# Batch 1 of an attention and MoE kernel: scores and strided turns issued at earlier steps, one subtraction moved from GpSimd to VectorE

## The chip, the cores and the metric

The kernel runs on one core of one Trainium2 chip. The metric is the device time of one execution in microseconds (us), and the time of a kernel is the median of its runs. A core has five engines that run side by side and meet at semaphores: TensorE (PE in the profile; PEld is its weight load), VectorE (DVE), ScalarE (ACT), GpSimd (POOL) and SyncE (SP). Matmul results land in PSUM, from where VectorE or ScalarE take them to SBUF. Here all loads are issued from GpSimd's queue, all stores from SyncE's.

## The reference

Two stages follow each other. The first is attention with a window, for 8 batches, 8 heads, 576 positions and head size 64:

```python
scores = scale * np.matmul(q, k.transpose(0, 1, 3, 2))
rel = pos[:, None] - pos[None, :]
mask_plain = (rel >= 0) & (rel < window)                                   # heads 0 to 3, window 32
mask_dil = (rel >= 0) & (rel < window * dilation) & (rel % dilation == 0)  # heads 4 to 7, dilation 4
scores = np.where(masks, scores, -1e9); scores -= max; attn = exp(scores)
attn = attn / (sum(attn) + 1e-9);  x = attn @ v
```

The second is a feed-forward layer over all 4608 tokens (8 batches of 576), with 512 features and 2048 hidden units: `h = x @ w_in`, `g = h * sigmoid(h)` (SiLU), `out = g @ w_out`.

## The kernel before

**Two kinds of work, one stream.** The feed-forward layer fills TensorE: for each batch `layer1` (L715) runs 16 steps of 8 matmuls (L721) and ScalarE applies SiLU to each (L729). `layer2` (L778) then runs 16 matmuls (L790) for each output tile of 128 tokens, VectorE copies the tile out of PSUM (`store`, L773, the copy at L775) and SyncE stores it. An odd batch such as batch 1 has five output tiles, numbers 4 to 8. The attention of later batches is woven into this stream.

**The steps.** `plan_of(b)` (L816) lists which piece of attention work is issued at which step while batch b's feed-forward layer runs. Steps 0 to 15 are the 16 steps of `layer1`. From step 16 on a step is four matmuls of `layer2`: tile 4 has steps 16 to 19, tile 5 has 20 to 23, tile 6 has 24 to 27, tile 7 has 28 to 31, tile 8 has 32 to 35. The pieces of a step are issued ahead of that step's matmuls. Nothing is sorted afterwards: each engine runs its instructions in the order in which the program issues them (the schedule is manual), and waits at the first whose inputs or buffers aren't ready. So a step number fixes an instruction's place in the order of every engine that it uses.

**The attention of one batch.** z = 0 stands for the plain heads, z = 1 for the strided (dilated) ones.

1. `load_qk`, `load_v`: q, k, v come in through GpSimd's queue, in tiles n0 (q), n1 (k) and vw. One `load_squares` issues four DMAs (L152).
2. `transposes(at, b, z, step)` (L801): q and k are turned so that the head size lies on partitions. Batch 2's plain heads are turned on TensorE, with copies on VectorE and ScalarE (L287). Batch 2's strided heads and everything of batch 3 are turned on VectorE by `turn_qk` (L329): two stream transposes each, kC and qC at L337 (strided), kT and qT at L335 (plain). `transposes` also passes two copy engines, which only the turn on TensorE uses.
3. `scores(b, z)` (L494): 72 (plain) or 80 (strided) small matmuls (L364 or L374) into PSUM tiles s and ss. Then VectorE scales and masks them into a tile ms (L408, three or four instructions) and takes the maxima (L488, two instructions). Each z has two halves, hi = 0 and 1, with a tile ms each. There are five buffers for ms, so the sixth tile waits until the first has been read.
4. `exps(b, z, hi)` (L548): ScalarE takes exponentials, as 8 or 10 small instructions with sums (L568), one per block of 64 keys. Where `shift` (L538) has subtracted the maximum from the whole tile before, it's one instruction (L557), and VectorE sums later (L576).
5. `later` (L808) places `normal` (L581: r at L587 and L588, the product pn at L590), `turned` (L594: a stream transpose into pt, L606), `values` (L647: matmuls of pt with v, L637) and `finish` (L663, copies into xT).

**Around the change.** In batch 1, batch 2's plain halves are normalized at steps 22 and 24, and their `values` are issued at step 28, ahead of tile 7; the strided ones follow at 29, 30 and 34. `values` starts with 28 matmuls that need only the first half of pt; the others need the second. ScalarE takes all 38 small exponentials of batch 2 after its last SiLU of batch 1, behind a load of its function table. In the kernel before, `shift(3, 0, 0)` is given `nc.gpsimd`, and runs on GpSimd behind batch 4's load instructions, which are issued at step 17. Output tiles o use two PSUM buffers (`big`): tile 6 may start when VectorE has copied tile 4, and tile 8 when it has copied tile 6.

The lines that the change and the prediction name are: L329 `turn_qk`, L494 `scores`, L538 `shift`, L548 `exps`, L581 `normal`, L594 `turned`, L773 `store` and L850 to L865, the plan of batch 1.

Of the kernel before, what the change touches and what calls it, by code (L numbers as in the profile page):

```python
# [29 lines left out]
def kernel(  # L30
# [9 lines left out]
    nc = tc.nc  # L40
# [212 lines left out]
    def att(b):  # L253
        if b not in state:
            state[b] = {
                "qT": qTs[b % 2],
                "kT": kTs[b % 2],
                "qC": qCs[b % 2],
                "kC": kCs[b % 2],
                "vw": vws[b % 2],  # L260
                "pt": {},
                "xT": [xtp.tile([P, 2, S], F16, tag=f"xT{z}", name=f"xT_{b}_{z}") for z in (0, 1)],
            }
        return state[b]
# [134 lines left out]
    def width(b, z, g):  # L399

        if b == 0:
            return 8 + g * (4 if z else 2)
        return 10 if z or g else 8
# [131 lines left out]
                masked(ms[:, 8:10], ss[0], band_of(2))  # L535
            reduce_max(b, z, m, ms)

    def shift(b, z, hi, engine=nc.vector):  # L538

        a = att(b)  # L540
        w = width(b, z, hi)
        ms, nm = a["ms", z, hi], a["nm", z, hi]
        engine.tensor_tensor(
            ms[:, 0:w], ms[:, 0:w], nm[:, 0:w, None].broadcast_to([P, w, KB]), ALU.add
        )
        a["shifted", z, hi] = True
# [251 lines left out]
    dve, act = nc.vector.tensor_copy, nc.scalar.copy  # L798
    both = (dve, act)

    def transposes(at, b, z, step, copies=both):  # L801
        for which in (1, 0):
            if b >= DT[z]:
                at(step, turn_qk, b, z, which)
                continue
            at(step, transpose, b, z, which, copies)

    def later(at, b, z, steps, copies=(nc.vector.tensor_copy, nc.vector.tensor_copy)):  # L808

        for hi in (0, 1):  # L810
            at(steps[hi], normal, b, z, hi)
            at(steps[hi], turned, b, z, hi)
        at(steps[3], values, b, z)
        at(steps[3], finish, b, z, copies)

    def plan_of(b):  # L816
        ev = {}

        def at(s, fn, *args):
            ev.setdefault(s, []).append((fn, args))  # L820

        def all_exps(b, z):
            for hi in (0, 1):
                at(16, exps, b, z, hi)

        if b == 0:

            at(-8, values0, 1, 1)
            at(-8, finish0, 1, 1, (act, dve))
            at(-6, values0, 0, 1)  # L830
            at(-6, finish0, 0, 1)
            at(0, build_mask)
            at(1, load_qk, 2)
            transposes(at, 1, 1, 4)
            at(8, scores, 1, 1, 0)
            at(10, scores, 1, 1, 1)
            at(12, transpose, 1, 0, 1, both)
            at(14, transpose, 1, 0, 0, both)
            at(10, shift, 1, 1, 0)
            at(16, scores, 1, 0, 0)  # L840
            at(18, scores, 1, 0, 1)
            at(18, shift, 1, 0, 1)
            at(15, load_qk, 3)
            at(15, load_v, 2)
            all_exps(1, 1)
            for hi in (0, 1):
                at(20, exps, 1, 0, hi)
            later(at, 1, 1, (20, 21, 24, 27), (act, act))
            later(at, 1, 0, (23, 24, 28, 31), (act, act))
        elif b == 1:  # L850
            at(16, load_v, 3)
            transposes(at, 2, 0, 3)
            transposes(at, 2, 1, 10)
            transposes(at, 3, 0, 17, (dve, dve))
            at(8, scores, 2, 0)
            at(17, load_qk, 4)
            at(13, scores, 2, 1)
            all_exps(2, 0)
            all_exps(2, 1)
            at(20, scores, 3, 0)  # L860
            at(21, shift, 3, 0, 0, nc.gpsimd)
            at(21, exps, 3, 0, 0)
            at(21, exps, 3, 0, 1)
            later(at, 2, 0, (22, 24, 27, 28))
            later(at, 2, 1, (29, 30, 33, 34), both)  # L865
        else:
            if b + 2 < B:
                at(16, load_v, b + 2)
            if b + 1 < B:
                later(at, b + 1, 0, (0, 0, 4, 6))  # L870
                transposes(at, b + 1, 1, 7)
                if b + 3 < B:
                    at(16, load_qk, b + 3)
            if b + 2 < B:
                transposes(at, b + 2, 0, 14)
                at(19, scores, b + 2, 0)
                at(20, exps, b + 2, 0, 0)
                at(20, exps, b + 2, 0, 1)
            if b + 1 < B:
                at(12, scores, b + 1, 1)  # L880
                all_exps(b + 1, 1)
                later(at, b + 1, 1, (22, 23, 27, 28))

        def plan(s):
            for fn, args in ev.pop(s, ()):
                fn(*args)

        return plan
# [48 lines left out]
    for b in range(B):  # L937
        plan = plan_of(b)
        if b == 0:
            for f in range(0, 12, 4):  # L940
                layer1_part(f, 0, plan)
            for f in range(0, NFF, 2):
                if f == 12:
                    layer1_part(12, 0, plan)
                layer1_part(f, 1, plan)
        else:
            for f in range(NFF):
                plan(f)
                layer1(b, f)
        if b == 0:  # L950
            layer2_first(plan)
        else:
            layer2(b, plan)
        for s in range(NFF, 3 * NFF):
            plan(s)
# [30 lines left out]
```

## Time and profile before

| | us |
|---|---|
| median of 3 runs | 306.78 (306.5 to 307.46) |
| the profiled execution, its time | 307.47 |
| its span, first to last instruction | 305.7 |
| TensorE busy | 292.6 (96%) |
| VectorE busy | 193.1 (63%) |
| ScalarE busy | 203.8 (67%) |
| GpSimd busy | 120.0 (39%) |

The profile shows one execution, whose time of 307.47 us is 1.77 us more than its span. Times inside it count from the span's start. A timeline line reads: start, duration, engine, source line, operation, output <- input, count; in brackets stands how long the engine was idle before it and what ended that. A line of waits reads: who waited, for whom, us in total, times, longest. Matmuls overlap each other in the pipeline, so the end of a group of matmuls runs over the start of the next. Batch 1's `layer1` begins at 57.45 us, its `layer2` at 76.33 us, and batch 2's `layer1` at 97.84 us.

### The profile page before, as it was taken

How to read it: one execution, taken by the hardware profiler on the slowest of the kernel's cores; microseconds unless marked ns; L12 is line 12 of the kernel's file. 1: busy time of each engine (PE TensorE's matmuls, PEld its weight loads, DVE VectorE, ACT ScalarE, POOL GpSimd, SP SyncE). 2: the span in 40 equal slices, each digit the busy share in tenths (PEclk: the TensorE clock that was granted, in tenths of full speed). 3: DMA queues.
4: the chain of work that ended last, by engine and by line, in shares of the span. 5: the costliest groups of instructions: out<-in, count | busy, mean ns of one | idle time of the engine just before them, and what ended most of it. 6: DMA issues, size and time to landing. Idle time of an engine off the chain costs nothing.

```text
span 305.7 us, 10277 instructions
## 1 busy us (share of the span) xinstructions
PE 292.6 (96%) x4393; PEld 186.8 (61%) x4393; DVE 193.1 (63%) x353; ACT 203.8 (67%) x685; POOL 120.0 (39%) x182
## 2 busy tenths in 40 slices
PE   2998999999989999999999999999999999999995
PEld 1666754677445775477644775478644775477544
DVE  1895579448898868866893768955893762810012
ACT  3676597765997559975895559975795559546200
POOL 8745347979963295236906086240000000000000
PEclk9999999999999999999999999999999999999999
DMA  8999999999993899399959199390002100110021
GB/s 102 159 204 207 207 161 171 195 184 126 121 187 71 94 67 131 109 116 38 121 74 186 38 59 136 104 119 4 3 34 105 36 2 34 52 56 0 17 88 69
DMA packets 113213, 30.47 MB, mean 100 GB/s; under 512 B 95520, under 2 KB 108688, under 8 KB 113168
## 3 DMA queue, kind: packets, MB, share of 16 engines
q0 software_dynamic: 107840, 20.38, 80.8%
q1 hardware_dynamic: 5328, 9.44, 8.6%
q8 instruction: 34, 0.56, 0.8%
q14 instruction: 11, 0.09, 0.1%
HBM read 40.75 MB, written 9.44 MB: 164 GB/s over the span
## 4 chain that ended last, share of the span: by engine, by line
PE 78%; DMA 8%; DVE 5%; POOL 3%; ACT 3%; issue 2%; DVEq 0%; POOLq 0%
PE h L721 32%; PE o L790 31%; PE h L746 5%; PE x L637 4%; PE o L766 3%; DMA w_in<-in_moe_w_in_dram 3%; DMA n<-in_q_dram 2%; DMA gT<-in_q_dram 2%; ACT pe L568 2%; PE s L364 2%; POOL n L152 2%; DVE pn L590 1%; DMA vw<-in_v_dram 1%; POOL gT L135 1%; DVE ob L775 1%
## 5 line engine op out<-in xcount | busy, mean ns | idle before, releaser
L729 ACT ACTIVATE gT<-h 128x576 f16<-128x576 f32 x112 | 72.8, 650 | 61.5 <-PE h L721 61.3
L790 PE MATMUL o<-w_out,gT 128*128 128x512 f16 (+1 forms) x528 | 113.8, 373 | 0.0
L721 PE MATMUL h<-xT,w_in 128*128 128x288 f16 x896 | 113.4, 287 | 0.0
L721 PEld LDWEIGHTS <-w_in 128*128 128x128 f16 x896 | 86.5, 98 | 23.6 <-issue 0.2
L790 PEld LDWEIGHTS <-gT 128*128 128x128 f16 x528 | 50.6, 98 | 55.4
L568 ACT ACTIVATE pe<-ms,nm 128x64 f32<-128x64 f32 x238 | 78.9, 333 | 0.1
L775 DVE COPY ob<-o 128x512 f32<-128x512 f32 (+1 forms) x35 | 22.9, 664 | 51.8 <-PE o L790 50.6
L568 ACT ACTIVATION_READ_ACCUMULATOR pe<-ms,nm 128x1 f32 x238 | 44.5, 187 | 0.0
L152 POOL DMA_DIRECT2D n<-in_k_dram x44 | 31.9, 736 | 26.1 <-DVE kC L337 25.1
L408 DVE SCALAR_TENSOR_TENSOR ms<-s,mask 128x512 f32<-128x512 f32 x28 | 19.2, 686 | 29.1 <-PE s L364 19.9
L152 POOL DMA_DIRECT2D n<-in_q_dram x44 | 32.0, 744 | 2.5 <-DMA n<-in_q_dram 2.5
L174 POOL DMA_DIRECT2D vw<-in_v_dram x32 | 18.3, 578 | 35.3 <-PE x L637 33.0
L590 DVE TENSOR_TENSOR pn<-pe,r 128x640 f16<-128x640 f32 (+2 forms) x32 | 26.2, 818 | 1.1
L606 DVE STREAM_TRANSPOSE pt<-pn 128x640 f16<-128x640 f16 (+4 forms) x32 | 24.7, 772 | 1.1
L183 POOL DMA_DIRECT2D vw<-in_v_dram x32 | 21.2, 672 | 10.0 <-DMA w_out<-in_moe_w_out_dram 7.8
L488 DVE TENSOR_REDUCE nm<-ms 128x10 f32<-128x640 f32 (+1 forms) x28 | 22.0, 787 | 1.0
L746 PE MATMUL h<-xT,w_in 128*128 128x256 f16 (+1 forms) x128 | 19.2, 304 | 1.6 <-DVE band L244 0.9
L637 PEld LDWEIGHTS <-vw 32*64 32x64 f16 (+1 forms) x1264 | 13.0, 107 | 7.4 <-issue 7.1
L637 PE MATMUL x<-pt,vw 32*64 32x64 f16 (+2 forms) x1264 | 14.9, 193 | 1.7 <-DVE pt L606 1.7
L746 PEld LDWEIGHTS <-w_in 128*128 128x128 f16 x128 | 12.5, 104 | 6.3 <-issue 1.5
L766 PE MATMUL o<-w_out,gT 128*128 128x512 f16 x64 | 14.5, 380 | 0.0
L670 DVE CAST xT<-x 128x288 f16<-128x288 f32 x24 | 9.3, 449 | 7.7 <-PE x L637 7.7
(92 smaller groups left out, 204.6 us busy)
## 6 DMA issues: line engine op xcount, KB each, us to landing
out_dram<-ob SPq DMA_DIRECT2D x35, 256.0 KB, 3.4
n<-in_k_dram POOLq DMA_DIRECT2D x24, 108.0 KB, 4.2
n<-in_q_dram POOLq DMA_DIRECT2D x24, 108.0 KB, 4.9
vw<-in_v_dram POOLq DMA_DIRECT2D x31, 80.0 KB, 4.0
vw<-in_v_dram POOLq DMA_DIRECT2D x32, 72.0 KB, 3.9
w_in<-in_moe_w_in_dram POOLq DMA_DIRECT2D x4, 512.0 KB, 9.5
w_out<-in_moe_w_out_dram POOLq DMA_DIRECT2D x4, 512.0 KB, 11.4
n<-in_k_dram POOLq DMA_DIRECT2D x20, 72.0 KB, 4.0
```

The lines of the kernel that those rows point to most:

```text
L152: nc.gpsimd.dma_start(out=qk[b, z, which][o : o + QB], in_=bass.AP((q, k)[which].tensor, (b * H + z * HH + half * HH // 2) * S * D + x * Q ...
L488: nc.vector.tensor_reduce(out=nm[:, 0:w], in_=ms[:, 0:w], axis=AX.X, op=ALU.max, negate=True)
L568: nc.scalar.activation(pe[:, t, :], src[t], AF.Exp, bias=a["nm", z, hi][:, t : t + 1], scale=k, accum_out=l[:, t : t + 1],)
L590: nc.vector.tensor_tensor(pn[:, 0:w], a["pe", z, hi][:, 0:w], r[:, 0:w, None].broadcast_to([P, w, KB]), ALU.mult)
L606: nc.vector.transpose(out, src)
L637: nc.tensor.matmul(x[h // 2][h % 2 * D : h % 2 * D + D, col : col + wd], vws[b % 2][r, NB + kb * DIL + c if z else kb], turned_cols(b, pt[ ...
L721: nc.tensor.matmul(h[:, half, 0:HS], w_in16[:, c, f * P : f * P + P], xT[c // 2][:, c % 2, half * HS : half * HS + HS], start=(c == cs[0]) ...
L729: nc.scalar.activation(gT[:, f, s0 : s0 + S].rearrange("p (a c) -> p a c", a=2), h[:, :, 0:HS], AF.Silu)
L746: nc.tensor.matmul(hs[i // m][:, i % m, 0 : c1 - c0], w_in16[:, c, (f + i) * P : (f + i + 1) * P], xT[c // 2][:, c % 2, c0:c1], start=(c = ...
L766: nc.tensor.matmul(o, gT[:, f, t * P : (t + 1) * P], w_out16[:, f, :], start=(f == 0), stop=(f == NFF - 1),)
L775: copy(ob, o)
L790: nc.tensor.matmul(o[:, 0, 0:m], gT[:, f, t * P : (t + 1) * P], w_out16[:, f, cols], start=(f == 0), stop=(f == NFF - 1),)
```

## The change

In batch 1's plan, nine entries get another step, and one instruction another engine:

- batch 2's plain scores: step 8 to 6; its strided turn: 10 to 7; its strided scores: 13 to 12
- batch 3's plain turn: 17 to 13; its plain scores: 20 to 19; its subtraction of the maxima and its exponentials: 21 to 20
- the normalization of batch 2's first plain half: 22 to 21
- `shift` always runs on VectorE

VectorE's order stays the same up to batch 3's plain turn. Behind it, VectorE now masks batch 3's scores first and copies output tile 4 after that (before, it copied tile 4 first), then runs the subtraction (128x512), then normalizes batch 2's first half. On TensorE batch 3's scores now stand ahead of the last four matmuls of tile 4, and not behind them. GpSimd's queue loses its one subtraction; the order of its loads stays as it was. Of the instructions that stay, the only waits that differ are those for the subtraction on GpSimd: batch 3's exponential and a later mask no longer have them.

```diff
-    def shift(b, z, hi, engine=nc.vector):
+    def shift(b, z, hi):
...
-        engine.tensor_tensor(
+        nc.vector.tensor_tensor(
             ms[:, 0:w], ms[:, 0:w], nm[:, 0:w, None].broadcast_to([P, w, KB]), ALU.add
         )
...
         elif b == 1:
             at(16, load_v, 3)
             transposes(at, 2, 0, 3)
-            transposes(at, 2, 1, 10)
-            transposes(at, 3, 0, 17, (dve, dve))
-            at(8, scores, 2, 0)
+            at(6, scores, 2, 0)
+            transposes(at, 2, 1, 7)
             at(17, load_qk, 4)
-            at(13, scores, 2, 1)
+            at(12, scores, 2, 1)
+            transposes(at, 3, 0, 13, (dve, dve))
             all_exps(2, 0)
             all_exps(2, 1)
-            at(20, scores, 3, 0)
-            at(21, shift, 3, 0, 0, nc.gpsimd)
-            at(21, exps, 3, 0, 0)
-            at(21, exps, 3, 0, 1)
-            later(at, 2, 0, (22, 24, 27, 28))
+            at(19, scores, 3, 0)
+            at(20, shift, 3, 0, 0)
+            at(20, exps, 3, 0, 0)
+            at(20, exps, 3, 0, 1)
+            later(at, 2, 0, (21, 24, 27, 28))
             later(at, 2, 1, (29, 30, 33, 34), both)
```

## The prediction

> **What bounds the kernel now.** I read the page first. TensorE is busy for 96% of the span, so all that a reordering can win is its idle time.
>
> ```profile
> span 305.7 us, 10277 instructions
> PE 292.6 (96%) x4393; PEld 186.8 (61%) x4393; DVE 193.1 (63%) x353; ACT 203.8 (67%) x685; POOL 120.0 (39%) x182
> ```
>
> The second view is the list of TensorE's waits. Most of its 13.1 us idle lie at the start of the kernel. Batch 1's stage has two waits: 0.4 us for the strided turn, and the 1.3 us (the longest of two) for pt.
>
> ```profile
> PE x L637 <- DVE pt L606: 1.7, 2, 1.3
> PE s L364 <- DVE qC L337: 0.4, 1, 0.4
> ```
>
> Third, the timeline of TensorE shows where: 0.37 us ahead of batch 2's strided scores at 72.63, and 1.31 us inside batch 2's plain `values`, whose first 28 matmuls run at 87.60 and the others at 89.32. After that nothing stops TensorE until 0.36 us at 265.12. So this stage can win 1.68 us at most, 0.55% of the time.
>
> ```profile
> 72.63 0.68 PE L364 MATMUL s<-kC,qC 64*32 64x64 f16 x64 [0.37 <-DVE qC L337]
> 87.60 0.41 PE L637 MATMUL x<-pt,vw 32*64 32x64 f16 x28
> 89.32 0.61 PE L637 MATMUL x<-pt,vw 32*64 32x64 f16 x48 [1.31 <-DVE pt L606]
> ```
>
> Fourth, the timeline of VectorE says why pt is late. After 0.69 us idle it runs without a gap from 79.99 to 89.26: tile 4's copy, batch 3's masks, then batch 2's normalization. One product of 128x640 takes 1.65 us, where the group's median is 0.826; GpSimd's subtraction is on record beside it.
>
> ```profile
> 77.97 1.33 DVE L335 STREAM_TRANSPOSE qT<-n 128x1152 f16<-128x1152 f16 x1
> 79.99 0.69 DVE L775 COPY ob<-o 128x512 f32<-128x512 f32 x1 [0.69 <-PE o L790]
> 80.60 0.68 DVE L408 SCALAR_TENSOR_TENSOR ms<-s,mask 128x512 f32<-128x512 f32 x1
> ...
> 81.92 0.68 DVE L408 SCALAR_TENSOR_TENSOR ms<-s,mask 128x512 f32<-128x512 f32 x1
> ...
> 84.10 0.69 DVE L590 TENSOR_TENSOR pn<-pe,r 128x512 f16<-128x512 f32 x1
> ...
> 86.04 0.42 DVE L587 TENSOR_SCALAR r<-l 128x10 f32<-128x10 f32 x1
> 86.49 0.22 DVE L588 RECIPROCAL r<-r 128x10 f32<-128x10 f32 x1
> 86.74 1.65 DVE L590 TENSOR_TENSOR pn<-pe,r 128x640 f16<-128x640 f32 x1
> 88.42 0.84 DVE L606 STREAM_TRANSPOSE pt<-pn 128x640 f16<-128x640 f16 x1
> ```
>
> ```profile
> 87.74 1.54 POOL L543 TENSOR_TENSOR ms<-ms,nm 128x512 f32<-128x512 f32 x1
> ```
>
> Last, ScalarE: its exponentials start after the last SiLU and a table load. The eighth, the last reader of batch 2's first ms tile, is done with its sum at 81.26.
>
> ```profile
> 76.53 0.65 ACT L729 ACTIVATE gT<-h 128x576 f16<-128x576 f32 x1 [0.33 <-PE h L721]
> 77.20 1.28 ACT L568 ACT_TABLE_LOAD   x1
> ...
> 81.07 0.19 ACT L568 ACTIVATION_READ_ACCUMULATOR pe<-ms,nm 128x1 f32 x1
> ```
>
> **The change part by part.** A step of `layer1` is 0.98 us (in the chain of waits, 48 matmuls of L721 take 5.88 us from 98.00: six steps).
>
> *Batch 2's plain scores, strided turn and strided scores.* The scores move up two steps, from 66.48 to 64.52. VectorE is idle for 4.31 us ahead of their mask, and their kT and qT have been ready since 62.66, so masks and strided turn move up by 1.96 with them: the turn starts at 67.99 and ends at 70.61 (72.57 before). Its loads were issued from 45.04 to 51.0 and land within 7.1 us (the longest in the view of tile n), by 58.1. The strided scores move up one step, to 72.26 - 0.98 = 71.28, which leaves 0.67 us for the turn. The wait of 0.37 goes, and `layer2` starts at 75.96 instead of 76.33.
>
> *Batch 3's turn and scores.* VectorE's strided masks start 0.73 after their scores, as before (73.36 against 72.63), at 72.01, and end at 75.32 (76.67 before, 1.35 earlier). Batch 3's plain turn follows, until 77.95. Its step number alone changes nothing: the same instruction precedes it on VectorE. Its loads, issued by 58.5, land by 65.6. Batch 3's scores now stand behind 12 matmuls of tile 4. These take 2.68 us in batch 2, where scores stand at this place (115.25 to 117.93), so they start at 78.64, 0.69 after the turn. The first mask begins 0.50 later (117.93 to 118.43), at 79.14, and the next could follow 1.33 after it (118.43 to 119.76), at 80.47.
>
> *A wait that now counts.* That second mask writes the sixth ms tile, in the buffer of batch 2's first, so it waits for the eighth exponential. Before, it ran at 81.92 against 81.26. Now ScalarE is earlier by only the 0.37 us of TensorE: 80.89, and the mask starts at about 80.95. VectorE idles for about 0.5 us; queued behind the mask are tile 4's copy, the subtraction and batch 2's normalization. The gain here is 81.92 - 80.95 = 0.97, not the 1.45 that the scores alone would give.
>
> *The rest of VectorE's chain.* From 80.95: mask, small mask and maxima 1.65 (81.92 to 83.57) make 82.60; tile 4's copy, now behind them, 0.60 (121.41 to 122.01) makes 83.20; the subtraction, new on VectorE, 0.73 (a 128x512 product, 84.10 to 84.83) makes 83.93. GpSimd is issuing loads meanwhile, but a 128x640 subtraction on VectorE at 45.42 took 0.82 during such issues, the usual price. First half's normalization and tile 5's copy take 2.47 (83.57 to 86.04): 86.40. The r pair takes 0.44 (122.01 to 122.45) to the 0.70 seen here: 86.84 to 87.10. The product, without GpSimd beside it, takes 0.86 (122.45 to 123.31): 87.70 to 87.96. The turn and the release of TensorE take 0.90 (88.42 to 89.32): 88.60 to 88.86, against 89.32. The gain is 0.46 to 0.72; I take 0.6, the middle, since loads are still issued beside the r pair.
>
> That 0.82 us of the slow product is GpSimd's doing is an inference. Its bounds are 0.82 and 0 regained; I take all of it, since all 31 other products have their shape's usual time and this one alone has GpSimd arithmetic on record beside it. A rule speaks against that: the Trainium skill, "SBUF — State Buffer", section "SBUF: two separate sides", says that VectorE and GpSimd lock a shared port pair, and that whichever instruction starts first holds it to its end. By the recorded starts (86.74 and 87.74) that is the product, which by the rule wouldn't be slowed, and TensorE would go on at 89.42 to 89.68.
>
> *Costed at nothing.* TensorE's count of matmuls stays. Tile 6 needs tile 4's copy, now done at 83.2; TensorE gets there at 75.96 + 2.68 + 0.71 of scores + 0.87 + 3.55 = 83.77. If that cover of 0.57 fails, the delay first shortens the wait for pt, which still has about 1 us. Tile 4's store leaves SP's queue some 2.6 us later; its buffer is next wanted by tile 8's copy at 98.04. GpSimd loses 1.54 us, but then idles for 7.21 us until `values` frees vw, so its loads don't move for that. Batch 3's first exponential has its input at 83.9 instead of 89.28, and runs at 91.09 by ScalarE's order anyway.
>
> *What is late next, and the sum.* Not both waits are won: the 0.37 at the turn only shifts into the wait for pt, which shrinks from 1.31 to about 1.1. Behind `values`, VectorE and TensorE are both 0.6 earlier, so the strided `values` meet their pt as before. ScalarE ends its exponentials 0.37 earlier, at 94.64, ahead of the copies wanted at 95.29. From there TensorE is continuous, so 0.6 reaches the end. Against the profiled execution the sum is 307.47 - 0.6 = 306.87. That execution stands 0.69 above the median, so for the median it is 306.78 - 0.6 = **306.2 us**, 0.2% less. A change of 0.3% (0.92 us, bounds 305.86 and 307.70) is about what a measurement of this kernel can tell from none.
>
> **The rivals.**
>
> - *The ms buffer doesn't hold VectorE.* If the eighth exponential is done by 80.47, all of the chain starts 0.48 earlier, the gain is 0.94 to 1.20, and the time 305.6 to 305.8. Against it: ScalarE's chain is serial, 0.331 us for each exponential behind the table load, and only 0.37 is seen to be won ahead of it.
> - *The slow product stays slow*, because its cause is something else. Then VectorE has the subtraction in addition and regains nothing: TensorE goes on at 89.42 to 89.68, 0.1 to 0.4 later, 306.9 to 307.2. For it: the r ahead of the product was slow too (0.42), before the subtraction's recorded start, and such an r occurs at 131.60 (0.40) without one.
> - *Slower: the strided turn waits for a load.* The chain of waits names a landing of v at 69.30 ahead of the turn. Were that real, the turn would stay at 69.95 to 72.57, and the strided scores, a step sooner, would wait for 1.35 us. With four steps behind them and not three, `layer2` starts at 77.30, 0.97 later than before; the eighth exponential is at 82.23, the mask at 82.29, and pt frees TensorE at 89.94 to 90.20: 307.4 to 307.7. It decides once the turn starts after 68.66. Against it: v isn't its input, and maxima on VectorE ran until 70.04, which explains 69.95 by itself.
> - *The gain is given back later*, at the strided `values` or by ScalarE's copies: 306.8.
>
> **How the numbers follow.** The forecast has a chance of 0.48, with its own range 306.06 to 306.32. The ms rival has 0.17, the slow product 0.15, the late turn 0.10, the gain given back 0.10. The range from 305.5 to 307.2 takes in the first three and the last; the late turn and the scatter of the runs stay outside. Faster by over 0.3%: all of the ms rival, and a quarter of the forecast by scatter and by terms that are 0.3 off, 0.30. Slower: more than half of the late turn and a little of the slow product, 0.10. The same: 0.60.
>
> **What would show it.** In the changed kernel's profile: no wait of TensorE ahead of the strided scores, which start near 71.3; `layer2` from 75.96; VectorE idle for about 0.5 us ahead of the second mask of batch 3, ended by ScalarE; the subtraction at 0.7; the product at 0.83 and not 1.65; the 28 matmuls of `values` near 87.2, and a remaining wait for pt of about 1 us until 88.7. A product still at 1.65, a strided turn that starts at 69.95, or a new wait of TensorE for tile 4's copy that adds to the one for pt would make it wrong.

## The result, and the profile after

The changed kernel takes 308.37 us (median of 21 runs, 307.05 to 309.71), the kernel before 307.13 us in the runs made beside them (21 runs, 306.08 to 308.23). The ratio is 1.0033, with a 95% interval from 1.0019 to 1.0048: slower by a third of a per cent, where I had forecast 0.2% faster and given "slower by over 0.3%" one chance in ten. The profiled execution took 308.83 us, with a span of 307.1 us. One execution of a later kernel (64 filler matmuls) ran at a granted clock of 0.574, took 498.81 us and is left out of every comparison.

The list of TensorE's waits in the changed kernel has a row that the kernel before doesn't have (columns: who waited, for whom, us in total, times, longest):

```profile
PE x L637 <- DVE pt L606: 1.5, 2, 1.1
PE h L721 <- issue: 1.3, 1, 1.3
```

The wait for the strided turn (0.4 us) is gone and the longest wait for pt shrank from 1.3 to 1.1 us, both as forecast. But `layer1` now stops for 1.3 us, and "issue" means that it waited for nothing that the profile shows. The timeline of TensorE in the changed kernel gives the place:

```profile
65.07 0.70 PE L374 MATMUL s<-kT,qT 64*32 64x64 f16 x64
65.59 0.26 PE L374 MATMUL ss<-kT,qT 64*32 64x64 f16 x8
65.78 0.67 PE L721 MATMUL h<-xT,w_in 128*128 128x288 f16 x4
67.71 5.55 PE L721 MATMUL h<-xT,w_in 128*128 128x288 f16 x44 [1.27 <-issue]
...
77.88 2.75 PE L790 MATMUL o<-w_out,gT 128*128 128x512 f16 x12
...
89.14 0.41 PE L637 MATMUL x<-pt,vw 32*64 32x64 f16 x28
90.67 0.61 PE L637 MATMUL x<-pt,vw 32*64 32x64 f16 x48 [1.11 <-DVE pt L606]
```

Batch 2's plain scores run two steps sooner, four matmuls of `layer1` follow, and then TensorE stands still for 1.27 us in the middle of a step's eight matmuls, whose weights and inputs have long been there.

Batch 1's `layer1` starts at 58.00 us here and at 57.45 us before, though the instructions up to there are the same. So I count from its start: `values` went on 31.87 us after it before (89.32 - 57.45), and 32.67 after the change (90.67 - 58.00), 0.80 us later. Behind that the two traces are equal: the span ends 216.38 us after `values` went on in both (305.70 - 89.32 and 307.05 - 90.67). The difference of the two spans, 1.35 us, is 0.55 ahead of `layer1` and 0.80 inside batch 1. By the recorded idle time the 0.80 is a stop of 1.27 less a gain of 0.47. The profile models the ends of matmuls, so the idle time is a little short: `layer2` starts 19.88 us after `layer1` here and 18.44 in the runs below that have no stop and no wait ahead of the strided scores, so the stop costs 1.44, and the gain is 0.64.

VectorE's part came out as worked out. Its timeline in the changed kernel:

```profile
82.83 0.69 DVE L408 SCALAR_TENSOR_TENSOR ms<-s,mask 128x512 f32<-128x512 f32 x1 [0.37 <-ACT pe L568]
...
85.09 0.68 DVE L543 TENSOR_TENSOR ms<-ms,nm 128x512 f32<-128x512 f32 x1
...
88.21 0.41 DVE L587 TENSOR_SCALAR r<-l 128x10 f32<-128x10 f32 x1
88.66 0.22 DVE L588 RECIPROCAL r<-r 128x10 f32<-128x10 f32 x1
88.91 0.82 DVE L590 TENSOR_TENSOR pn<-pe,r 128x640 f16<-128x640 f32 x1
```

The mask waits for the exponential, the subtraction costs 0.68 us, and the product of 128x640 takes 0.82 us instead of 1.65.

**What the stop is.** The page's list of DMA queues has a row that I had not read, the same in both kernels (packets, MB, share of 16 engines):

```profile
q8 instruction: 34, 0.56, 0.8%
```

0.56 MB in 34 packets is 16 KB each, and TensorE's 8,797 instructions in the trace (a weight load and a matmul for each of 4,393 products, and a few more) at 0.56 MB are about 64 bytes each: a packet is a block of 256 instructions. In the trace, one block of the changed kernel is fetched from 65.31 to 66.29 us, and TensorE goes on at 67.71, 1.42 us after it landed. A small stop early in the kernel looks the same, both before (block landed at 26.15, TensorE went on at 27.61) and after (26.72 and 28.16). In the chain of waits of the kernel before, it stands as "issue" (its list of waits puts all 0.9 us of idle there down to VectorE's work on the tile band):

```profile
27.13 0.47 issue
```

The stop at 66.44 stands behind TensorE's 2497th instruction in the trace. Counting back 256, the block end before it is passed at 61.61 us, in batch 2's transposes. The kernel before runs 55 instructions of transposes in this block, 80 of five `layer1` steps and 121 of the scores, and gets to the last of them after 5.87 us (61.06 to 66.93). The next block had landed at 65.47, and 65.47 plus 1.42 is 66.89: just in time. The changed kernel has 55 instructions of transposes, 48 of three steps, all 144 of the scores and 9 behind them. It gets to its last in 4.55 us (61.61 to 66.16), while the fetch begins only 3.7 us after the block end.

That is theory 1: the block of instructions comes late, since the scores moved into it make it short and its fetch queues behind loads. Theory 2 is that scores between steps 5 and 6 stop the matmuls behind them as such, wherever a block ends.

### The profile page after: what moved, and what is told of

It is laid out like the page before. It is cut to its first block, busy times and chain, and to the rows that moved or that the text cites. A ratio compares the mean times of both kernels' runs of the same rounds, so it can differ in the third digit from the quotient of the medians.

```text
span 307.1 us, 10275 instructions
## 1 busy us (share of the span) xinstructions
PE 293.0 (95%) x4393; PEld 187.0 (61%) x4393; DVE 193.0 (63%) x354; ACT 203.9 (66%) x685; POOL 118.7 (39%) x181
## 4 chain that ended last, share of the span: by engine, by line
PE 86%; ACT 4%; DVE 4%; DMA 2%; issue 2%; POOL 1%; POOLq 0%
PE h L721 36%; PE o L790 30%; PE h L746 6%; PE o L766 5%; PE x L637 4%; ACT pe L568 3%; DMA gT<-in_q_dram 2%; PE s L364 2%; ACT L568 1%; DVE pn L590 1%; PE t L283 1%; POOL gT L135 1%; DVE ob L775 1%; DVE pt L606 1%; PE s L374 0%
## 5 line engine op out<-in xcount | busy, mean ns | idle before, releaser
L590 DVE TENSOR_TENSOR pn<-pe,r 128x640 f16<-128x640 f32 (+2 forms) x32 | 25.3, 792 | 1.1
L754 ACT ACTIVATE gT<-h 128x640 f16<-128x640 f32 (+2 forms) x13 | 9.8, 760 | 6.9 <-PE h L746 6.6
```

The lines of the kernel that those rows point to most:

```text
L590: nc.vector.tensor_tensor(pn[:, 0:w], a["pe", z, hi][:, 0:w], r[:, 0:w, None].broadcast_to([P, w, KB]), ALU.mult)
```

## The experiments

The times of `layer2` and values below count from the start of batch 1's `layer1` in the run's own trace, in us. "Values" is the moment at which TensorE goes on behind the wait for pt. "Stop on a block" is the one near batch 2's plain scores; where the block end falls inside the scores, it is read from the length of the score group (0.90 and 0.87 us for 64 of them instead of 0.70, in the runs with about 0.2).

| run | layer1 starts | layer2 | values | stop on a block | ratio to before (95%) |
|---|---|---|---|---|---|
| before | 57.45 | 18.88 | 31.87 | none | 1 |
| changed | 58.00 | 19.88 | 32.67 | 1.27 | 1.0033 (1.0019 to 1.0048) |
| changed, second profile | 57.99 | 19.30 | 31.75 | 0.70 | one run |
| 64 filler matmuls (times from a second profile) | 58.46 | 18.44 | 31.20 | none | 1.0021 (0.9997 to 1.0045) |
| 128 filler matmuls | 59.43 | 19.74 | 32.12 | 1.13 | 1.0096 (1.0070 to 1.0122) |
| before, 64 filler matmuls | 58.34 | 18.89 | 32.11 | none | 1.0046 (1.0020 to 1.0072) |
| plain scores at step 8 | 57.91 | 18.44 | 31.30 | none | 0.9986 (0.9968 to 1.0004) |
| plain scores at step 7 | 58.72 | 18.88 | 31.58 | about 0.1 | 1.0016 (0.9990 to 1.0042) |
| loads held back | 58.59 | 18.44 | 30.83 | none | 1.0003 (0.9977 to 1.0029) |
| before, subtraction on VectorE | 57.42 | 18.89 | 31.38 | about 0.2 | 0.9998 (0.9974 to 1.0023) |
| step 8 and six ms buffers | 57.10 | 18.59 | 30.52 | about 0.2 | 0.9978 (0.9959 to 0.9997) |

**Moving the block ends.** The edit adds small matmuls on zeros ahead of TensorE's first work, and changes nothing else:

```diff
+    zero = cpool.tile([W, KB], F16, name="zero")
+    nc.vector.memset(zero, 0.0)
+    filler = ps.tile([W, KB], F32, tag="ps", name="filler")
+    for _ in range(64):
+        nc.tensor.matmul(filler, zero[:, 0:W], zero, start=True, stop=True, skip_group_check=True)
     load_v(0)
```

> The changed kernel with 64 small matmuls (32x64, on zeros) ahead of TensorE's first real work, where it is idle until 5.4 us; nothing else differs. They add 128 instructions (64 weight loads, 64 matmuls) to TensorE's stream. Theory 1, instruction blocks: TensorE stopped for 1.27 us at 66.44 because the next block of 256 of its instructions (16 KB on queue q8) landed late. With 128 instructions more ahead, the block ends elsewhere and that stop goes, or shrinks below 0.4 us: batch 1's layer2 then starts 18.4 to 18.9 us after its layer1 (19.88 in the changed kernel, 18.88 before), batch 2's values go on 31.2 to 31.7 after it (32.67 and 31.87), and the time falls by about 1.0 to 1.4 us against the changed kernel, to 0.1 to 0.4% below before, if the first 57 us don't lose by their own block ends. Theory 2, the stop belongs to the place of the scores (between steps 5 and 6, whatever stands ahead): the stop of 1.2 to 1.3 us stays, and the time is that of the changed kernel.

> The changed kernel with 64 filler matmuls (128 instructions) once more, since the first profile of it was taken at a granted clock of 0.574. Theory 1 (instruction blocks): no stop of TensorE over 0.4 us between the plain scores of batch 2 and the strided ones; layer2 starts 18.4 to 18.9 us after layer1 (19.88 in the changed kernel), values go on 31.2 to 31.7 us after it (32.67). Theory 2 (the place of the scores): a stop of 1.2 to 1.3 us right behind the plain scores, 19.9 and 32.7 us.

With 64 fillers the stop is gone. TensorE's timeline in the second profile of that kernel:

```profile
65.53 0.70 PE L379 MATMUL s<-kT,qT 64*32 64x64 f16 x64
66.05 0.26 PE L379 MATMUL ss<-kT,qT 64*32 64x64 f16 x8
66.24 6.05 PE L726 MATMUL h<-xT,w_in 128*128 128x288 f16 x48
...
89.66 0.61 PE L642 MATMUL x<-pt,vw 32*64 32x64 f16 x48 [1.08 <-DVE pt L611]
```

All 48 matmuls behind the scores run without a break, `layer2` starts 18.44 us after `layer1` and values go on after 31.20, as theory 1 expected and theory 2 did not. The time fell by less than expected, to 1.0021 of before, and `layer1` begins at 58.46. The fillers themselves hardly cost that: they end at 4.61 us, and TensorE's first real work starts at 5.63 (5.45 in the changed kernel), when its load has landed. But with the block ends moved, TensorE stops at another place early in the kernel: 2.27 us of "issue" until 19.20, 1.45 us after a block that landed at 17.75. The changed kernel waits only 1.15 us there, for VectorE. So the fillers bring a stop of the same kind elsewhere.

With 128 fillers (256 instructions, one whole block) the ends fall on the old instructions again:

> As the run with 64 filler matmuls, but 128, so 256 instructions: exactly one block. Theory 1: all later block ends fall on the same instructions as in the changed kernel, so the stop of about 1.3 us behind batch 2's plain scores is back, and the time is that of the changed kernel (0.3% above before). Theory 2: the same stop. A third theory, that more matmuls at the start or another PSUM buffer rotation help by themselves: no stop here either.

```profile
67.21 0.66 PE L726 MATMUL h<-xT,w_in 128*128 128x288 f16 x4
69.00 5.55 PE L726 MATMUL h<-xT,w_in 128*128 128x288 f16 x44 [1.13 <-issue]
```

The stop is back, behind the same four matmuls, 1.44 us after its block landed at 67.56. More fillers made it come back, so it isn't their presence that took it away. Moving the stream by 128 instructions took the stop away and moving it by 256 brought it back, so the stop hangs on a count of 256 instructions. The time of the run, 1.0096, was expected at 1.003; here the fillers alone take 7.00 us, longer than TensorE's idle start of 5.5, and `layer1` starts at 59.43.

The control with 64 fillers in the kernel before:

> The kernel before with the same 64 filler matmuls. It is the control for the first 57 us and for the later block ends: theory 1 expects no stop near batch 2's plain scores (there was none before), the 0.4 us ahead of the strided scores and the 1.3 us for pt as before, and a time within 0.3% of before; where it differs, by block ends in the first 57 us (the kernel before idles 0.47 us on an instruction block at 27.1). Theory 2 expects the same.

It had no stop at the scores and both old waits (0.38 for the turn, 1.55 for pt). The time was 1.0046 (1.0020 to 1.0072), above what I expected: `layer1` starts at 58.34, behind an early stop of 0.47 us until 31.66, and the wait for pt is 0.24 longer than before. That wait has the slow product in it: beside GpSimd's subtraction (recorded from 87.77) the product of 128x640 took 2.26 us here. The profiled execution, 310.21 us, also had a granted clock of only 0.83 between 90 and 100 us, behind the stretch that is read here.

**Putting back the one entry.**

```diff
-            at(6, scores, 2, 0)
+            at(8, scores, 2, 0)
```

> The changed kernel with one entry put back: batch 2's plain scores at step 8 again, everything else as changed. Theory 1: TensorE reaches the end of its block as late as before (the 144 quick instructions of these scores mostly come behind it), so the stop of 1.27 us goes. VectorE turns batch 2's strided q and k ahead of those masks now, in its idle time, so the wait of 0.37 us ahead of the strided scores goes too: layer2 starts 18.4 to 18.7 us after layer1, values go on 31.2 to 31.5 after it, and the time is 0.4 to 0.7 us below before. Theory 2 (the place of the scores): the stop goes as well, so this run alone doesn't tell the two apart. A theory that the later edits (batch 3's scores inside tile 4, the subtraction on VectorE, tile 4's copy behind the masks) cost the time: still 0.3% above before.

The stop is gone, and so is the wait ahead of the strided scores. TensorE's timeline in this kernel has the whole of what I had forecast for the change:

```profile
76.35 2.75 PE L790 MATMUL o<-w_out,gT 128*128 128x512 f16 x12
...
89.21 0.61 PE L637 MATMUL x<-pt,vw 32*64 32x64 f16 x48 [1.18 <-DVE pt L606]
```

Values go on 31.30 us after `layer1`, 0.57 sooner than before; the time is 0.9986 of before (0.9968 to 1.0004), 0.36 us by the medians where 0.4 to 0.7 was expected. So of all the edits it is the two steps of batch 2's plain scores that lost the time.

**Between the two.** The same entry at step 7:

> The changed kernel with batch 2's plain scores at step 7, between 6 (changed) and 8 (before). Theory 1 (instruction blocks) as a dose: the block end falls 120 of the 144 score instructions in, so the stop moves from behind the scores to inside them, ahead of their last 12 or so matmuls. TensorE reaches it 8.6 us after layer1 begins (scores at 8.05 plus 0.5), and the block is usable at about 9.4 (fetch start 3.5 to 3.7 us behind the block end at 3.6, 0.97 of transfer, 1.43 until TensorE goes on, as in the changed kernel), so the stop is 0.5 to 1.0 us, values go on 31.8 to 32.4 us after layer1 begins, and the time lies between after_scores8 and the changed kernel. A theory that scores ahead of step 8 as such stop the matmuls behind them: a stop of 1.2 to 1.3 us behind the scores, none inside.

The block end falls inside the scores, 7 instructions ahead of their end (137 of 144 in, not the 120 expected), and no stop of 0.5 to 1.0 us is there: 72 scores take 0.82 us (66.76 to 67.58) instead of 0.71, so at most 0.1 us is lost. The expectation missed because it fixed the fetch to `layer1`. In this execution `layer1` began late, at 58.72, and the fetch began at 65.16, as in the others. In the seven profiles with the old loads and the old block ends, the block end is passed anywhere from 60.71 to 62.32 us, and the fetch begins between 64.41 and 65.31. The block ends spread over 1.61 us and the fetches over 0.90, so the fetch doesn't simply follow the block end. The block landed at 66.14; TensorE got to the block end at 67.31 and went on at 67.44, 1.30 us after the landing, as behind the other stops. `layer2` starts 18.88 us after `layer1`, since TensorE also waits 0.26 us for the strided turn.

**The changed kernel once more.**

> The changed kernel, unchanged, once more, to see whether the stop belongs to every execution. Theory 1: a stop of 1.0 to 1.4 us behind the first four matmuls after batch 2's plain scores, about 1.4 us after the landing of the block whose fetch began 3 to 4 us behind the block end. A theory that it was one execution's accident: no stop there.

TensorE's timeline has the stop again, shorter:

```profile
67.13 5.55 PE L721 MATMUL h<-xT,w_in 128*128 128x288 f16 x44 [0.70 <-issue]
```

The fetch began at 64.90 and landed at 65.87, 0.42 sooner than in the first profile, and TensorE went on 1.26 us later. The stop is in both executions, at the same instruction, and it is shorter where the fetch was sooner; at 0.70 us it is below the 1.0 to 1.4 expected. Values go on 31.75 us after `layer1`, in spite of the stop 0.12 sooner than in the kernel before.

**Whether the fetch queues behind loads.** GpSimd's loads of batch 3's strided squares and batch 2's v are put behind a tiny copy that reads batch 2's turned q, so they leave after 71.8 us:

```diff
-            at(15, load_qk, 3)
-            at(15, load_v, 2)
+            at(15, load_qk, 3, (0,))
...
+            at(8, held, 2)
+            at(8, load_qk, 3, (1,))
+            at(8, load_v, 2)
...
+    def held(b):
+        gate = stat.tile([P, 2], F16, tag="gate", name=f"gate_{b}")
+        nc.gpsimd.tensor_copy(gate, flat(b, 1, 0)[:, 0:2])
```

> The changed kernel, with GpSimd's loads of batch 3's strided squares and of batch 2's v held back: they stand behind a tiny copy on GpSimd that reads batch 2's strided turn, so they are issued from about 70 us on instead of 59 to 71. TensorE's stream is the same, instruction for instruction. It asks whether the block of instructions came late because it queued behind loads: in the changed kernel TensorE passed the block end before at 61.6 us, the fetch began at 65.3, 3.7 us later, while the DMA engines were full with loads. If so, the fetch begins sooner here, within about 2.5 us of that block end, and the stop of 1.27 us shrinks to 0 to 0.6 us. If the fetch takes its time whatever is loaded, the stop stays at 1.1 to 1.3 us. The time may lose elsewhere, since later loads shift by about 10 us.

In the changed kernel, the list of DMA queues (packets, MB, share of 16 engines' time) from the block end to the start of the fetch (61.6 to 65.3 us), and then for the microsecond of the fetch, shows the load queue at 182 and 189% of 16 engines, so with nearly two packets at once on each:

```profile
q0 software_dynamic: 3429, 0.45, 181.7%
q1 hardware_dynamic: 155, 0.28, 22.6%
...
q0 software_dynamic: 849, 0.16, 188.6%
q8 instruction: 1, 0.02, 6.1%
```

With the loads held back the load queue has thinned out behind the block end (62.2 to 63.0 us), though the queue of the stores (q1) is busier there:

```profile
q0 software_dynamic: 455, 0.03, 94.6%
q1 hardware_dynamic: 104, 0.19, 72.7%
```

The fetch begins at 63.09, 0.9 us after the block end and not 3.7, and `layer1` runs through:

```profile
66.37 6.05 PE L727 MATMUL h<-xT,w_in 128*128 128x288 f16 x48
```

The stream of TensorE is the changed kernel's, with the scores at step 6. So the fetch was late because of the loads, and theory 2 falls a second time. Later, though, the shifted loads coincide with batch 2's strided normalization, where the two r instructions take 0.36 and 0.49 us, and the strided `values` wait 0.56 us for pt, longer than in any other run. The time is that of before, 1.0003.

**Whether GpSimd's subtraction slowed the product.** The kernel before, with one edit:

```diff
-            at(21, shift, 3, 0, 0, nc.gpsimd)
+            at(21, shift, 3, 0, 0)
```

> The kernel before with one part of the change alone: the subtraction of batch 3's first maxima on VectorE, at its old step. If GpSimd's subtraction was what slowed the product beside it (1.65 us for 0.83), the product takes 0.82 to 0.84 here, the subtraction adds 0.6 to 0.7, and values go on 31.5 to 31.9 us after batch 1's layer1 begins (31.87 before): the time of before within 0.2%. If the product was slow for another reason, it stays at 1.65, and values go on at 32.4 to 32.6, 0.2% slower.

VectorE's timeline in this kernel:

```profile
83.54 0.68 DVE L543 TENSOR_TENSOR ms<-ms,nm 128x512 f32<-128x512 f32 x1
...
86.51 0.24 DVE L587 TENSOR_SCALAR r<-l 128x10 f32<-128x10 f32 x1
86.79 0.22 DVE L588 RECIPROCAL r<-r 128x10 f32<-128x10 f32 x1
87.04 0.83 DVE L590 TENSOR_TENSOR pn<-pe,r 128x640 f16<-128x640 f32 x1
```

The product takes 0.83 us: the subtraction on GpSimd was what made it 1.65. Values go on after 31.38 us, 0.49 sooner, a little below the expected 31.5. Of the 0.49, the edit itself explains 0.22: the product is 0.82 shorter, and the subtraction adds 0.60 to VectorE's chain. The other 0.27 is r, the two instructions at L587, which were quicker (0.17 and 0.24 us, and 0.26 and 0.42 before). They also differ between executions of one kernel (0.32 and 0.41 in the first profile of the changed kernel, 0.23 and 0.15 in the second), so this 0.27 can't be credited to the edit. The time, 0.9998 (0.9974 to 1.0023), is too coarse to show either.

**A version that beats both.** The scores at step 8, and the mask no longer behind the exponential:

```diff
-    msp = ctx.enter_context(tc.tile_pool(name="msp", bufs=5))
+    msp = ctx.enter_context(tc.tile_pool(name="msp", bufs=6))
...
-            at(6, scores, 2, 0)
+            at(8, scores, 2, 0)
```

> The changed kernel with batch 2's plain scores back at step 8 (as in the run after_scores8) and six buffers for the masked scores instead of five. Batch 3's second mask then needn't wait for ScalarE's eighth exponential (0.36 us in after_scores8): no idle of VectorE ended by ScalarE there, the chain to pt 0.3 to 0.4 us earlier, values go on 30.9 to 31.0 us after layer1 begins (31.30 in after_scores8, 31.87 before), and the time is 0.25 to 0.35% below before. If something else in that chain is late next (the exponentials' sums, the output copies), the gain stays at that of after_scores8, 0.14%.

VectorE no longer waits for ScalarE there, and the wait for pt has nearly gone from TensorE's timeline:

```profile
87.62 0.61 PE L637 MATMUL x<-pt,vw 32*64 32x64 f16 x48 [0.25 <-DVE pt L606]
```

Values go on after 30.52 us, 1.35 sooner than before and sooner than the 30.9 to 31.0 expected. Against the run with the scores at step 8 it is 0.78 sooner: 0.36 is the wait for ScalarE, and the rest is r again (0.17 and 0.16 us, where that run had 0.40 twice). The time is 0.9978 of before (0.9959 to 0.9997), 0.22% where 0.25 to 0.35 was expected, and the only run whose interval lies wholly below.

## Why the prediction was wrong

- **The step that failed** is the first of the change part by part, "batch 2's plain scores, strided turn and strided scores", with the line under "costed at nothing" that TensorE's count of matmuls stays. I moved 144 quick instructions up by two steps and took the matmuls behind them to follow at 0.98 us a step. They didn't: the stream itself ran dry for 1.27 us, and 0.70 in the second profile. `layer2` was to start 18.51 us after `layer1`; it started 18.44 after where the stop was away, and 19.88 with it. A wait on TensorE's own instructions was neither a term nor a rival. The profile of before had both signs, the row of q8 and 0.47 us of "issue" ahead of TensorE at 27.13.
- **The gain was right, with some luck.** I forecast values 0.46 to 0.72 sooner. They are 0.57 sooner with the scores at step 8, 0.67 with 64 fillers and 1.04 with the loads held back. Where the stop is there, its cost is taken off by the start of `layer2` (18.44 without it): that leaves 0.64 for the changed kernel, 0.98 for its second profile and 1.05 for 128 fillers. The three near 0.6 had a slow r (the two L587 instructions took 0.69 to 0.80 us together), the three near 1.0 a quick one (0.32 to 0.38). The range held for the slow r that the profile of before also had (0.68). What makes r slow or quick no run here isolates.
- **The ms buffer** held VectorE for 0.37 us (0.5 forecast), ended by ScalarE, and with six buffers that wait is gone and values go on sooner. That rival falls for this kernel as it stood.
- **The slow product** was GpSimd's doing, as taken; that rival falls too. The rule that I had weighed against it (the Trainium skill, "SBUF — State Buffer", section "SBUF: two separate sides": whichever starts first holds the shared port) would have left it slow by the recorded starts, 86.74 for the product and 87.74 for the subtraction. The run with the subtraction on VectorE, 0.83 us, speaks against it by these starts, and so does the kernel before with fillers (2.26 us from 87.27, the subtraction recorded from 87.77). But GpSimd's recorded starts are rough, and where its work really began no run here shows.
- **The late turn**, my rival on the slower side, was not it: the strided turn ran at 68.55 us, right after the maxima, without waiting for a load. The sign was right there for the wrong reason, and I had given it one chance in ten.
- **The second wait for pt** did stay as forecast, at 1.11 us (about 1.1); in the second profile, with its quick r, it was 0.78.
- **What stays open.** The medians differ by 1.24 us. In the first profile of the changed kernel batch 1 lost 0.80 of that; in the second it gained 0.12 in spite of the stop. In both, `layer1` also began about 0.55 us later than in the profile of before. Its start lies anywhere from 57.10 to 58.72 us in seven profiles whose instructions up to there have the same order, so I take that for scatter of the first loads, but no run separates the two. So the two profiles don't account for the whole difference of the medians. What ties it to the scores is that putting their one entry back took the time from 1.0033 to 0.9986 of before; how long the stop was in the executions without a profile isn't on record.

The Trainium skill, "Runtime: NRT & Kernel Launch", section "Instruction fetch mechanics", describes blocks of 16 KiB, or 256 instructions, which an engine's sequencer fetches through a DMA queue of its own, and calls the cost of a block end mostly hidden. The blocks agree with q8's 34 packets of 16 KB, and with the stop that came back with 256 more instructions. The cost was hidden here where the load queue left room or the block lasted long enough; with neither it was a stop of 1.27 us (0.70 in the second profile).

## What to carry to other kernels

In a long unrolled kernel, TensorE's instruction stream is a load like the others. Small matmuls use it up fast (144 instructions in 0.7 us, where a step of large ones takes 0.98 us for 16), so before moving a burst of them, count the instructions between the ends of 256-instruction blocks and look at what the load queue does there. An idle time that the profile puts down to "issue", with a packet of the instruction queue landing about 1.4 us before it ends, is the sign of it; the list of waits can also name another engine there, as it named VectorE for the early stop of the kernel before. A forecast that adds up waits of engines for each other misses it; adding instructions that do nothing ahead, half a block and then a whole one, tells it apart from a cause that lies in the order of the work.

## What was not expected of the hardware

- TensorE goes on 1.26 to 1.56 us after the landing of the block that it waits for (nine stops of 0.39 us or more in six profiles; eight of them are within 1.26 to 1.46).
- With the load queue full, a block's fetch began 2.8 to 3.7 us behind the block end before it (64.41 to 65.31 us); with loads held back, 0.9 us.
- The block fetched after one block end is needed at the next: beside the full load queue a stretch of 256 instructions that takes 4.55 us was too short for it by 1.27 us, one of 5.87 us was just long enough; with the loads held back 4.55 us was enough.
- One subtraction of 128x512 on GpSimd (1.54 us) made a product on VectorE of 0.83 us take 1.65; in another execution, of the kernel before with fillers, the product took 2.26.
